# Where the places and the channels lie: the state of a long convolution, stored by channel pairs or by places

## The chip, the cores and the metric

The kernel runs on one core of a Trainium2 chip. The metric is the device time of one execution in microseconds: the median of three runs. A separate execution was recorded by the hardware profiler, and all views of the profile below come from that one.

## The reference

Two blocks stand one behind the other. The first is a long convolution over the sequence, computed through Fourier transforms for 4 batches of 12,480 places and 128 channels; the second is a feed-forward block with the gate `h * cos(h)` for the 49,920 rows that come out of it. Everything is float32.

```python
def _attn_ref(x, v, pos_emb, w1, w2):
    B, S, D = x.shape                       # 4, 12480, 128
    h_mlp = np.maximum(pos_emb @ w1, 0.0) @ w2
    window = np.exp(-0.01 * np.arange(S, dtype=np.float32))[:, None]
    h_filt = h_mlp * window
    u = x * v
    L = 2 * S
    Uf = np.fft.rfft(u, n=L, axis=1)
    Hf = np.fft.rfft(h_filt, n=L, axis=0)
    y = np.fft.irfft(Uf * Hf[None, :, :], n=L, axis=1)[:, :S, :]
    return (x * y).astype(np.float32)

def _moe_ref(x, w_in, w_out):               # 49920 x 128, d_ff 2048
    h = x @ w_in
    g = h * np.cos(h)
    return (g @ w_out).astype(np.float32)
```

## The kernel before

**The convolution** is a transform in two steps, with tables of sines and cosines as matrices (N1 = 96, N2 = 120). The state of one batch is one tile in SBUF, `slots`: partitions, 64 pairs of channels (`b`, CB = 64), 240 places (`j`), and the two channels of a pair (`i`). Its partition axis is the axis that the next step contracts, and each step overwrites it:

- *u*: `u_units` multiplies x and v (L437) and writes sums and differences of them into `slots` (`u_sums`, L447). On the way out of memory nothing is rearranged.
- *f1*: `f1_mm` (L455) takes, for one channel, 64 or 60 places of `slots` as the stationary operand and the table `c1` as the moving one, 192 columns. `f1_evict` copies the result of a channel pair back to 192 places of that pair (L467, mostly on ACT). For the filter `f1_evict_filter` writes to a tile of its own, `ftile` (L474), and to `above`, the upper places of `slots` (L476).
- *f2*: `f2_mm` takes a table `w` as the stationary operand and, for one place, all 128 channels of two complex parts as the moving one, 256 columns. `f2_product` multiplies with the filter's transform `h` and writes back to the place (L504 or L508, L510, L511). In the first batch the filter's f2 (L488, L491) runs beside it, and its result goes to memory as `hd` and is loaded for the later batches.
- *i1*: `i1_mm` takes for one channel 96 places (97 in the long stage) as the stationary operand and the table `cs` as the moving one, 120 columns. `i1_evict` writes 240 places of a channel pair (L531, L533; in the first batch for some pairs L524 and L527).
- *i2*: `i2_mm` takes a table `t` (in the trace `tm`) as the stationary operand and all 128 channels of a place as the moving one. `i2_out` multiplies by x (L555) and stores rows to `zd`.

**The feed-forward block** reads blocks of 128 rows by 4 places from `zd`, turns them (`moe_turn`), multiplies by `w_in` in 16 pieces of 512 columns (`moe_up`, ph), makes the gate on ACT and DVE (L810, L811, L816, L817) and multiplies by `w_out` with seven products in place of eight (`moe_sums` on POOL, `moe_down` at L842, acca and accb).

**Order.** The whole order is written out by hand. The first batch's filter, f1, f2 and i1 run alone (to about 303 us); after that the flag `tiled[0]` is set and the loop over (block, piece) asks a generator for one small step of the convolution behind every piece of the feed-forward block. So from then on i2 of a batch, u, f1, f2 and i1 of the next are spread between the matmuls of the feed-forward block. With the flag set `mm` (L136) splits the stationary operand of a matmul into columns 0 to 64 and the rest, and issues two matmuls to the two halves of the array:

```python
def mm(dst, left, right, start=True, stop=True):
    n = dst.shape[0]
    for lo, hi in ((0, CB), (CB, n)) if tiled[0] else ((0, n),):
        nc.tensor.matmul(dst[lo:hi], left[:, lo:hi], right, start=start, stop=stop)
```

f1 is always issued in two such halves (64 and 60 places). Each float32 matmul of the code appears in the profile as two MATMUL records, each with a LDWEIGHTS record of its own; the counts below are those of the records. In the profile's names `cv` is a PSUM bank of the convolution in the long stage, `ps` one in the first stage, `even` the tile that then holds `cs`, and `c` the tile `c1`.

`Between` hands out unused places of `slots` as work tiles before the first f1. `aT`, the hidden layer of the filter, lies in the upper places as well.

Of the kernel before, what the change touches and what calls it, by code (L numbers as in the profile page):

```python
# [10 lines left out]
F32 = mybir.dt.float32  # L11
# [7 lines left out]
P = 128  # L19
BANK = 512  # L20
# [14 lines left out]
def kernel(  # L35
# [46 lines left out]
    nc = tc.nc  # L82
# [4 lines left out]
    N1, N2 = 96, 120  # L87
# [5 lines left out]
    KE = ODD + H  # L93
# [3 lines left out]
    FR = 2 * (2 * N2 - 2 * N1)  # L97
    KF = N1 - 2 * (N2 - N1)
    CB = D // 2
# [13 lines left out]
    WCOL = 256  # L113

    dram = ctx.enter_context(tc.tile_pool(name="dram", bufs=1, space=DRAM))
    hd = dram.tile([N1 // 2, N2, 2, CB, 4], F32, name="hd")
    zd = dram.tile([NROWS, G, D], F32, name="zd")
    wd = dram.tile([N1 // 2, KE, 2, N2], F32, name="wd")
    td = dram.tile([N2 // G, N1, G, 2, R], F32, name="td")
# [13 lines left out]
# [4 lines that stand above are left out]
# [66 lines left out]
    class Tables:  # L203
        def __init__(self, pool, engine):
            self.pool, self.engine, self.waiting = pool, engine, []
            self.prod, self.moved = (
                pool.tile([P, P], F32, name=name) for name in ("prod", "moved"))
# [88 lines left out]
    class Between:  # L296


        def __init__(self, slots, first, last):
            self.places, self.used = slots[:, :, first:last, :], 0  # L300

        def tile(self, shape, dtype, name=None, bufs=1):
            n = 1 if len(shape) == 2 else shape[1]
            rows = self.places[0:shape[0], self.used:self.used + n].rearrange(
                "p b j i -> p b (j i)")[:, :, 0:shape[-1]]
            self.used += n
            return rows if len(shape) == 3 else rows[:, 0]

# [2 lines left out]
    def last_tables(pool):  # L311
        rows = pool.tile([N1, 4, R], F32, name="rows")

        tw_t = pool.tile([N1, 2, N2], F32, name="tw_t")
        return rows, tw_t
# [18 lines left out]
    def make_w(w, k1, **how):  # L334


        turn(w, even[:, 0, :], even[:, 1, :], tw_w[:, 0, k1:k1 + 1], tw_w[:, 1, k1:k1 + 1],
             **how)
# [52 lines left out]
    def filter_out(bank, aT, slots, j, w2_sb):  # L391

        ps = bank()
        for i, (jj, step) in enumerate(((H - 1 - j, 2), (j, 1))):
            nc.tensor.matmul(ps[0:FR, i * 2 * D:(i + 1) * 2 * D], aT[:, jj, 0:FR],
                             w2_sb[:, 0:step + 1:step, :], start=True, stop=True)
        pj = ps[0:FR, :].rearrange("p (n s b i) -> p s b n i", n=2, s=2, i=2)
        a = H - 2 - 2 * j
        for i in range(2):
            place = i * ODD + a  # L400
            nc.scalar.copy(out=slots[0:FR, :, place:place + 2, :], in_=pj[:, i])

    def n2s(g):

# [17 lines left out]
    def clear_gap(u):  # L422

        nc.gpsimd.memset(u[:, :, H:ODD, :], 0.0)
# [54 lines left out]
    def f2_mm(ps, w, k1, i, filt=False):  # L479


        k = k1 + i
        pi = ps[0:N2, :].rearrange("p (r b g i) -> p g r b i", r=2, g=2, i=2)[:, i]
        if not filt:
            mm(pi, w[:, i, :], parts[0:KE, :, k])
        elif k < KF:
            both = ftile[0:KE, :, k:k + N1 + 1:N1, :].rearrange("p b r i -> p r b i")
            nc.tensor.matmul(pi, w[:, i, :], both, start=True, stop=True)  # L488
        else:
            for r, src in enumerate((ftile[0:KE, :, k, :], above[0:KE, :, k - KF, :])):  # L490
                nc.tensor.matmul(pi[:, r], w[:, i, :], src, start=True, stop=True)  # L491

    def f2_product(pool, ps, h, k1, whole, engine=nc.gpsimd):


        y = parts[0:N2, :, k1:k1 + 2, :, :].rearrange("p r k b i -> p r b (k i)")
        t = pool.tile([N2, 2, CB, 4], F32, name="t", bufs=2)
        uu = ps[0:N2, :].rearrange("p (r b j) -> p r b j", r=2, j=4)
        if whole:
            for r, (dst, hh) in enumerate(((y, h[:, :, :, :]), (t[:, :, :, :], h[:, ::-1, :, :]))):  # L500
                u = uu[:, r]
                twice = bass.AP(tensor=u.tensor, offset=u.offset,
                                ap=[u.ap[0], [0, 2], *u.ap[1:]])
                nc.vector.tensor_tensor(dst, twice, hh, op=ALU.mult)  # L504
                yield
        for r, op in ((0, ALU.subtract), (1, ALU.add)):
            if not whole:
                nc.vector.tensor_tensor(y[:, r], uu[:, 0], h[:, r], op=ALU.mult)  # L508
                yield
                nc.vector.tensor_tensor(t[:, r], uu[:, 1], h[:, 1 - r], op=ALU.mult)  # L510
            (engine if r else nc.gpsimd).tensor_tensor(y[:, r], y[:, r], t[:, r], op=op)  # L511
            yield
# [127 lines left out]
    def f2_units(bank):  # L640
        with tc.tile_pool(name="there", bufs=3) as pool:
            ws, hs = {}, {}

            def before(j):
                ws[j] = pool.tile([KE, 2, N2], F32, name="w")
                nc.sync.dma_start(ws[j][:, :, :], wd[j, :, :, :])
                hs[j] = pool.tile([N2, 2, CB, 4], F32, name="h")
                nc.sync.dma_start(hs[j][:, :, :, :], hd[j, :, :, :, :])

            def mm(j, ps, i):  # L650
                if i == 0:
                    ps = bank()
                f2_mm(ps, ws[j], 2 * j, i)
                return ps

            yield from units(N1 // 2, F2_STEPS, before, mm,
                             lambda j, ps: f2_product(pool, ps, hs.pop(j), 2 * j, False), 4)

    def f2_both_units(bank):

        with tc.tile_pool(name="both", bufs=2) as pool:
            ws = {}

            def before(j):
                ws[j] = pool.tile([KE, 2, N2], F32, name="w")
                for i in range(2):
                    make_w(ws[j][:, i, :], 2 * j + i, half=bank)
                nc.sync.dma_start(wd[j, :, :, :], ws[j][:, :, :])
                if j == N1 // 2 - 1:
                    nc.sync.dma_start(cs[:, :, :], csd[:, :, :])  # L670

            def mm(j, ps, i):
                if i == 0:
                    ps = bank(), bank()
                for k in range(2):
                    f2_mm(ps[1 - i], ws[j], 2 * j, k, filt=i == 0)
                return ps

            def after(j, ps):
                h = pool.tile([N2, 2, CB, 4], F32, name="h", bufs=3)  # L680
                nc.scalar.activation(h[:, :, :, :].rearrange("p r b j -> p (r b j)"),
                                     ps[1][0:N2, :], AF.Copy, scale=1.0 / M)
                nc.sync.dma_start(hd[j, :, :, :, :], h[:, :, :, :])
                last = j == N1 // 2 - 1
                yield from f2_product(pool, ps[0], h, 2 * j, not last,
                                      nc.vector if last else nc.gpsimd)

            yield from units(N1 // 2, F2_STEPS, before, mm, after, 4, ahead=1)
# [201 lines left out]
    with tc.manual_schedule():  # L890
        with tc.tile_pool(name="psum", bufs=8, space=PSUM) as psum, \
                ExitStack() as first:
            def bank():
                return psum.tile([P, BANK], F32, name="ps")

            spool = ctx.enter_context(tc.tile_pool(name="slots", bufs=1))
            slots = spool.tile([P, CB, 2 * N2, 2], F32, name="slots")
            parts = slots[:, :, 0:2 * N1, :].rearrange("p b (r k) i -> p r k b i", r=2)
            above = slots[:, :, 2 * N1:2 * N2, :]
            aT = above.rearrange("p b j i -> p b (j i)")  # L900


            keep = tc.tile_pool(name="keep", bufs=1)
# [1 line left out]
            with tc.tile_pool(name="layers", bufs=1, side="right") as pool:  # L905
# [6 lines left out]
                for i in range(1, NCH):  # L912
                    pes[i] = filter_load(pool, i)
                    if i == 3:
                        for m in range(2):
                            for n in range(2):
                                nc.sync.dma_start(
                                    w2_sb[m * FO:(m + 1) * FO, (m + 1) * n, :], w2[:, :])
                between = Between(slots, KE, 2 * N1)
                vs = [between.tile([R, 2 * UA, D], F32).rearrange("p (h n) d -> p h n d", h=2)  # L920
                      for _ in range(5)]
                xpool = tc.tile_pool(name="x", bufs=5)
# [37 lines left out]
                nc.scalar.activation(c1[:, 2, :], c1[:, 0, :], AF.Copy, scale=-1.0)  # L960

            fpool = first.enter_context(tc.tile_pool(name="ftile", bufs=1, side="right"))
            ftile = fpool.tile([P, CB, N1 + KF, 2], F32, name="ftile")
            clear_gap(ftile[0:FR, :, :, :])
            for j in range(H // 2):
                filter_out(bank, aT, ftile, j, w2_sb)
# [36 lines left out]
            rows, tw_t = last_tables(wpool)  # L1003
# [64 lines left out]
        for i in range(len(steps) + LAG):  # L1068
# [5 lines left out]
            if i < len(steps):  # L1074
                n, c = steps[i]
# [52 lines left out]
```

## Time and profile before

| | |
|---|---|
| median of 3 runs | 3674.26 us (3673.73 to 3675.14) |
| the profiled execution's own time | 3673.78 us |
| its span, first to last instruction | 3671.2 us |
| mean granted clock of TensorE | 0.998 |
| busy DVE, POOL, ACT | 2811.3, 2757.7, 2229.7 us |
| MATMUL and LDWEIGHTS records | 40,810 each |
| DMA | 281.78 MB, mean 77 GB/s |

The profile is one execution. Engines: PE is TensorE's matmul, PEld its weight load, DVE is VectorE, ACT is ScalarE, POOL is GpSimd, SP issues the DMAs. A row of a group gives the source line, the engine and operation, out<-in by the program's names, the shapes, the count, then the busy time in us, the mean of one in ns, and the idle time before them with what ended it. For PE a shape such as 120*64 120x120 says: 120 partitions contracted, 64 columns of weights, 120 columns streamed. A row of the timeline gives the start in us, the time from the first start to the last end of the merged instructions, and their count. Matmuls are pipelined, so the length of one record is more than the pace at which they follow each other; the pace is the distance between starts.

In time, the parts of the profiled execution are: the filter and the f1 steps to about 145 us, both f2 of the first batch to about 245 us, i1 of the first batch from 245.6 to about 303 us, and then the long stage. In it, f1, f2, i1 and i2 of the later batches take turns.

### The profile page before, as it was taken

The numbers are of one execution on the slowest core, as the hardware profiler recorded it, in microseconds if no ns is written. First come the engines' busy times: TensorE is split into PE (matmuls) and PEld (weight loads), VectorE is DVE, ScalarE is ACT, GpSimd is POOL, SyncE is SP. The second block draws the span as 40 slices with busy tenths as digits, with TensorE's granted clock in tenths as the row PEclk, the third lists the DMA queues.
The fourth block names the chain that finished last, engine by engine and source line by source line (L and its number), as shares of the span: only waits on it lengthen the run. The fifth ranks groups of instructions, "written<-read, shape, count | busy, mean of one in ns | idle before, by whom it ended". The sixth has DMA issues, their size and how long they took to land.

```text
span 3671.2 us, 101732 instructions
## 1 busy us (share of the span) xinstructions
PE 3605.1 (98%) x40810; PEld 2553.1 (70%) x40810; DVE 2811.3 (77%) x5289; ACT 2229.7 (61%) x4482; POOL 2757.7 (75%) x3237
## 2 busy tenths in 40 slices
PE   8999999999999999999999999999999999999999
PEld 6777776666678776666677776766667786666666
DVE  7777885688887776688887776578887667777777
ACT  6657666656554556655655556665555446666666
POOL 7667996688864886688874887578884448878877
PEclk9999999999999999999999999999999999999999
DMA  7454540022213551022211562012220350000000
GB/s 193 123 159 134 161 136 26 23 70 72 73 42 102 163 148 29 22 71 71 71 37 47 162 172 69 13 53 74 68 72 16 91 166 22 19 24 19 19 25 14
DMA packets 219583, 281.78 MB, mean 77 GB/s; under 512 B 18778, under 2 KB 156514, under 8 KB 218986
## 3 DMA queue, kind: packets, MB, share of 16 engines
q1 hardware_dynamic: 219114, 275.29, 26.3%
q8 instruction: 324, 5.31, 0.6%
q14 instruction: 145, 1.19, 0.1%
HBM read 194.75 MB, written 80.46 MB: 75 GB/s over the span
## 4 chain that ended last, share of the span: by engine, by line
PE 85%; DVE 4%; ACT 1%; POOL 1%; issue 1%; DMA 0%; ACTq 0%; DVEq 0%; POOLq 0%; SPq 0%
PE ph L136 30%; PE cv L136 18%; PE accb L842 17%; PE acca L842 13%; PE cv L455 3%; PE cv L140 1%; DVE gt L817 1%; DVE gt L811 1%; PE ph L140 1%; ACT gt L810 1%; POOL ts L825 0%; DVE t L510 0%; ACT tile L873 0%; DVE slots L508 0%; POOL ts L828 0%
## 5 line engine op out<-in xcount | busy, mean ns | idle before, releaser
L810 ACT ACTIVATE gt<-ph 128x512 int32<-128x512 f32 (+1 forms) x1380 | 823.1, 596 | 1143.4 <-PE ph L136 1087.6
L811 DVE SCALAR_TENSOR_TENSOR gt<-ph,gt 128x512 f32<-128x512 f32 (+1 forms) x1380 | 948.2, 687 | 716.0 <-ACT gt L810 712.9
L825 POOL TENSOR_TENSOR ts<-gt 128x512 f32<-128x512 f32 (+2 forms) x784 | 1006.2, 1283 | 581.8 <-PE accb L842 566.1
L136 PE MATMUL ph<-at,w_in_sb 128*64 128x512 f32 (+1 forms) x5520 | 1426.4, 592 | 13.3 <-ACT tile L873 6.8
L816 ACT ACTIVATE gt<-gt 128x512 f32<-128x512 f32 (+1 forms) x1568 | 972.0, 620 | 3.5 <-DVE gt L811 2.8
L817 DVE TENSOR_TENSOR gt<-ph,gt 128x512 f32<-128x512 f32 (+1 forms) x1380 | 934.7, 677 | 0.0
L842 PE MATMUL accb<-ts,w_out_sb 128*64 128x128 f32 (+2 forms) x9408 | 649.8, 272 | 0.0
L829 POOL TENSOR_TENSOR ts<-gt,ts 128x256 f32<-128x256 f32 (+2 forms) x784 | 574.4, 733 | 61.5
L828 POOL TENSOR_TENSOR ts<-ts,gt 128x256 f32<-128x256 f32 (+2 forms) x784 | 574.3, 732 | 61.5
L842 PEld LDWEIGHTS acca<-gt,w_out_sb 128*64 128x64 f32 x6272 | 398.9, 137 | 267.4 <-issue 231.3
L842 PEld LDWEIGHTS accb<-ts,w_out_sb 128*64 128x64 f32 x9408 | 543.5, 137 | 0.0
L842 PE MATMUL acca<-gt,w_out_sb 128*64 128x128 f32 (+2 forms) x6272 | 479.3, 272 | 0.0
L842 PEld LDWEIGHTS accb<-gt,w_out_sb 128*64 128x64 f32 x3136 | 225.5, 137 | 253.9 <-issue 198.8
L136 PEld LDWEIGHTS ph<-at,w_in_sb 128*64 128x64 f32 x5520 | 353.6, 137 | 32.8 <-ACT tile L873 15.0
L511 POOL TENSOR_TENSOR slots<-slots,t 120x256 f32<-120x256 f32 x383 | 280.7, 739 | 122.8 <-DVE t L510 70.2
L136 PEld LDWEIGHTS cv<-slots,tm 96*64 96x64 f32 (+1 forms) x3840 | 243.6, 127 | 119.6 <-issue 114.3
L842 PE MATMUL accb<-gt,w_out_sb 128*64 128x128 f32 (+1 forms) x3136 | 311.2, 273 | 4.2 <-DVE ot L863 2.8
L842 PE MATMUL acca<-ts,w_out_sb 128*64 128x128 f32 (+1 forms) x3136 | 308.7, 272 | 1.4 <-POOL ts L828 1.2
L136 PE MATMUL cv<-slots,tm 96*64 96x128 f32 (+1 forms) x3840 | 274.7, 285 | 3.9 <-DVE slots L533 3.4
L136 PEld LDWEIGHTS cv<-even,slots 120*64 120x64 f32 (+1 forms) x3072 | 168.4, 125 | 60.8 <-issue 58.8
L842 PEld LDWEIGHTS acca<-ts,w_out_sb 128*64 128x64 f32 x3136 | 201.6, 137 | 2.4 <-POOL ts L828 2.1
L136 PE MATMUL cv<-slots,w 124*64 124x256 f32 (+1 forms) x1152 | 191.1, 406 | 1.9 <-ACT at L799 1.9
(136 smaller groups left out, 3741.0 us busy)
## 6 DMA issues: line engine op xcount, KB each, us to landing
h<-hd SPq DMA_DIRECT2D x144, 240.0 KB
tm<-td SPq DMA_DIRECT2D x96, 312.0 KB
xt<-in_x_dram SPq DMA_DIRECT2D x120, 208.0 KB
xs<-in_x_dram SPq DMA_DIRECT2D x120, 208.0 KB
zd<-xs SPq DMA_DIRECT2D x119, 208.0 KB
tile<-zd SPq DMA_DIRECT2D x96, 256.0 KB
vt<-in_v_dram SPq DMA_DIRECT2D x90, 208.0 KB
w<-wd SPq DMA_DIRECT2D x144, 116.2 KB
```

The source lines that it names most:

```text
L136: nc.tensor.matmul(dst[lo:hi], left[:, lo:hi], right, start=start, stop=stop)
L140: nc.tensor.transpose(dst, src, ident[0:n, 0:n])
L455: nc.tensor.matmul(dst[lo:hi], u[:, b, lo:hi, i], c1[0:u.shape[0], r:r + 2, :].rearrange("p r k -> p (r k)"), start=True, stop=True)
L511: (engine if r else nc.gpsimd).tensor_tensor(y[:, r], y[:, r], t[:, r], op=op)
L810: nc.scalar.activation(turns, ph[:, 0:m], AF.Identity, bias=phase)
L811: nc.vector.scalar_tensor_tensor(out=part, in0=ph[:, 0:m], scalar=phase, in1=turns, op0=ALU.add, op1=ALU.subtract)
L816: nc.scalar.activation(part, part, AF.Sin, scale=scale)
L817: nc.vector.tensor_tensor(part, ph, part, op=ALU.mult)
L825: nc.gpsimd.tensor_tensor(ts[:, 0:2, 0:half], gt[:, :, half:2 * half], gt[:, 0, 0:2 * half].rearrange("p (h n) -> p h n", h=2), op=ALU.sub ...
L828: nc.gpsimd.tensor_tensor(t[2], t[1], b11, op=ALU.add)
L829: nc.gpsimd.tensor_tensor(t[3], b21, t[2], op=ALU.subtract)
L842: nc.tensor.matmul(acc[h * CB:(h + 1) * CB, place, 0:r], w_out_sb[:, pair, weight, :], right[:, h * r:(h + 1) * r], start=(pair == 0 and i ...
```

## The change

The state becomes one tile of partitions, 240 places, 64 pairs, 2 channels: the 128 channels of a place stand side by side (512 bytes), and the places of a channel are 512 bytes apart. Before, the places of a pair were side by side (8 bytes from one to the next), and a place's pairs 1920 bytes apart. `ftile` is turned in the same way. `slots`, `parts` and `above` become views of the new tile with the old order of axes, so that most of the code that uses them stays as it is. The output of f2 in PSUM is written with the pairs of a place side by side, and `t`, `h` and `hd` follow that order. `aT` and the tiles of `Between` become plain contiguous rows. No instruction is added or taken away.

```diff
-    hd = dram.tile([N1 // 2, N2, 2, CB, 4], F32, name="hd")
+    hd = dram.tile([N1 // 2, N2, 2, BANK // 2], F32, name="hd")
...
-            self.places, self.used = slots[:, :, first:last, :], 0
+            self.places, self.used = slots[:, first:last, :, :].rearrange(
+                "p j b i -> p (j b i)").rearrange("p (a n) -> p a n", a=CB), 0
...
-            rows = self.places[0:shape[0], self.used:self.used + n].rearrange(
-                "p b j i -> p b (j i)")[:, :, 0:shape[-1]]
+            rows = self.places[0:shape[0], self.used:self.used + n, 0:shape[-1]]
...
-        pj = ps[0:FR, :].rearrange("p (n s b i) -> p s b n i", n=2, s=2, i=2)
+        pj = ps[0:FR, :].rearrange("p (n s b i) -> p s n b i", n=2, s=2, i=2)
...
-            nc.scalar.copy(out=slots[0:FR, :, place:place + 2, :], in_=pj[:, i])
+            nc.scalar.copy(out=slots[0:FR, :, place:place + 2, :].transpose([0, 2, 1, 3]),
+                           in_=pj[:, i])
...
-        pi = ps[0:N2, :].rearrange("p (r b g i) -> p g r b i", r=2, g=2, i=2)[:, i]
+        pi = ps[0:N2, :].rearrange("p (r g b i) -> p g r b i", r=2, g=2, i=2)[:, i]
...
-        y = parts[0:N2, :, k1:k1 + 2, :, :].rearrange("p r k b i -> p r b (k i)")
-        t = pool.tile([N2, 2, CB, 4], F32, name="t", bufs=2)
-        uu = ps[0:N2, :].rearrange("p (r b j) -> p r b j", r=2, j=4)
+        y = parts[0:N2, :, k1:k1 + 2, :, :].rearrange("p r k b i -> p r (k b i)")
+        t = pool.tile([N2, 2, BANK // 2], F32, name="t", bufs=2)
+        uu = ps[0:N2, :].rearrange("p (r n) -> p r n", r=2)
...
-            slots = spool.tile([P, CB, 2 * N2, 2], F32, name="slots")
-            parts = slots[:, :, 0:2 * N1, :].rearrange("p b (r k) i -> p r k b i", r=2)
+            state = spool.tile([P, 2 * N2, CB, 2], F32, name="slots")
+            slots = state[:, :, :, :].rearrange("p j b i -> p b j i")
+            parts = state[:, 0:2 * N1, :, :].rearrange("p (r k) b i -> p r k b i", r=2)
             above = slots[:, :, 2 * N1:2 * N2, :]
-            aT = above.rearrange("p b j i -> p b (j i)")
+            aT = state[:, 2 * N1:2 * N2, :, :].rearrange("p j b i -> p (j b i)").rearrange(
+                "p (a n) -> p a n", a=CB)
...
-                between = Between(slots, KE, 2 * N1)
+                between = Between(state, KE, 2 * N1)
...
-            ftile = fpool.tile([P, CB, N1 + KF, 2], F32, name="ftile")
+            ftile = fpool.tile([P, N1 + KF, CB, 2], F32, name="ftile")
+            ftile = ftile[:, :, :, :].rearrange("p j b i -> p b j i")
```

More of the change, by code (lines that the diff above doesn't have):

```diff
@@ L493, in f2_product @@
     def f2_product(pool, ps, h, k1, whole, engine=nc.gpsimd):
-        y = parts[0:N2, :, k1:k1 + 2, :, :].rearrange("p r k b i -> p r b (k i)")
-        t = pool.tile([N2, 2, CB, 4], F32, name="t", bufs=2)
-        uu = ps[0:N2, :].rearrange("p (r b j) -> p r b j", r=2, j=4)
+        y = parts[0:N2, :, k1:k1 + 2, :, :].rearrange("p r k b i -> p r (k b i)")
+        t = pool.tile([N2, 2, BANK // 2], F32, name="t", bufs=2)
+        uu = ps[0:N2, :].rearrange("p (r n) -> p r n", r=2)
         if whole:
-            for r, (dst, hh) in enumerate(((y, h[:, :, :, :]), (t[:, :, :, :], h[:, ::-1, :, :]))):
+            for r, (dst, hh) in enumerate(((y, h[:, :, :]), (t[:, :, :], h[:, ::-1, :]))):
                 u = uu[:, r]
@@ L646, in before @@
                 nc.sync.dma_start(ws[j][:, :, :], wd[j, :, :, :])
-                hs[j] = pool.tile([N2, 2, CB, 4], F32, name="h")
-                nc.sync.dma_start(hs[j][:, :, :, :], hd[j, :, :, :, :])
+                hs[j] = pool.tile([N2, 2, BANK // 2], F32, name="h")
+                nc.sync.dma_start(hs[j][:, :, :], hd[j, :, :, :])
             def mm(j, ps, i):
@@ L679, in after @@
             def after(j, ps):
-                h = pool.tile([N2, 2, CB, 4], F32, name="h", bufs=3)
-                nc.scalar.activation(h[:, :, :, :].rearrange("p r b j -> p (r b j)"),
+                h = pool.tile([N2, 2, BANK // 2], F32, name="h", bufs=3)
+                nc.scalar.activation(h[:, :, :].rearrange("p r n -> p (r n)"),
                                      ps[1][0:N2, :], AF.Copy, scale=1.0 / M)
-                nc.sync.dma_start(hd[j, :, :, :, :], h[:, :, :, :])
+                nc.sync.dma_start(hd[j, :, :, :], h[:, :, :])
                 last = j == N1 // 2 - 1
```

## The prediction

> **What bounds the kernel now.** I read the page first: parts 1 and 4, then the groups kept apart by shape, and last the timeline of TensorE inside the long stage.
>
> ```profile
> PE 3605.1 (98%) x40810; PEld 2553.1 (70%) x40810; DVE 2811.3 (77%) x5289; ACT 2229.7 (61%) x4482; POOL 2757.7 (75%) x3237
> PE 85%; DVE 4%; ACT 1%; POOL 1%; issue 1%; DMA 0%; ACTq 0%; DVEq 0%; POOLq 0%; SPq 0%
> ```
>
> TensorE is busy 98% of the span and carries 85% of the chain that ended last; no other engine is over 77%. So only what changes the pace of TensorE counts at once. That pace stands in the timeline, in the distance from the start of one row to the start of the next, divided by the count (rows of three stretches, about 750, 1055 and 1230 us, and one of 600 us):
>
> ```profile
> 600.24 0.82 PE L455 MATMUL cv<-c,slots 104*64 104x192 f32 x8
> 600.89 0.61 PE L842 MATMUL acca<-gt,w_out_sb 128*64 128x128 f32 x8
> ...
> 749.60 0.68 PE L136 MATMUL cv<-slots,w 124*56 124x256 f32 x4
> 750.10 0.40 PE L842 MATMUL accb<-gt,w_out_sb 128*64 128x128 f32 x4
> ...
> 1054.55 1.03 PE L136 MATMUL ph<-at,w_in_sb 128*64 128x512 f32 x4
> 1055.41 1.40 PE L136 MATMUL cv<-even,slots 120*64 120x120 f32 x24
> 1056.64 0.61 PE L842 MATMUL acca<-gt,w_out_sb 128*64 128x128 f32 x8
> ...
> 1230.64 1.17 PE L136 MATMUL cv<-slots,tm 96*40 96x128 f32 x16
> 1231.63 0.40 PE L842 MATMUL accb<-gt,w_out_sb 128*64 128x128 f32 x4
> 1231.85 0.83 PE L842 MATMUL accb<-ts,w_out_sb 128*64 128x128 f32 x12
> 1232.51 1.03 PE L136 MATMUL ph<-at,w_in_sb 128*64 128x512 f32 x4
> ```
>
> The two column halves that `mm` issues start 5 to 7 ns apart in the trace and run side by side, so a matmul costs half a pass here. From the starts in these rows: ph 0.86/4 = 215 ns, acc 0.66/12 = 55, i1 (cv<-even,slots) 1.23/24 = 51, f1 (cv<-c,slots) 0.65/8 = 81, f2 (cv<-slots,w) 0.50/4 = 125, i2 (cv<-slots,tm) 0.99/16 = 62. Over all their runs in the trace the medians are 214.5, 54.6, 51.4, 81.5, 120.8 and 61.3 ns. In columns per ns that is ph 2.39, acc 2.34, i1 2.33, f1 2.36, but f2 2.12 and i2 2.09. Only these two are slow, and only these two stream `slots` as the moving operand: 64 pieces of 8 bytes, 1920 bytes apart. In the first batch, where f2 runs as one tile of 120 columns, its pass takes 218 ns for the same 256 columns: 1.17 per ns, half of 2.35, so the pieces cost nothing there. They cost when two tiles stream at once.
>
> The weight loads are the other half of the reading:
>
> ```profile
> L136 PEld LDWEIGHTS ph<-at,w_in_sb 128*64 128x64 f32 x5520 | 353.6, 137 | 32.8 <-ACT tile L873 15.0 <-issue 7.0 <-PE ph L140 3.0
> L136 PEld LDWEIGHTS cv<-even,slots 120*64 120x64 f32 x1536 | 165.1, 138 | 22.9 <-issue 21.0 <-ACT ot L856 1.8
> L136 PEld LDWEIGHTS cv<-even,slots 120*33 120x33 f32 x1536 | 157.7, 111 | 37.9 <-issue 37.9
> L455 PEld LDWEIGHTS cv<-c,slots 104*64 104x64 f32 x768 | 105.9, 139 | 105.9 <-issue 66.9 <-ACT slots L467 13.9 <-ACT gt L816 13.3
> L136 PEld LDWEIGHTS ps<-even,slots 120*96 120x96 f32 x512 | 55.5, 174 | 3.4 <-POOL slots L511 3.4
> ```
>
> 64 weight columns take 137 ns side by side (ph) and 138 at 8 bytes' step (i1), so that step is free. From 33 to 64 columns is 27 ns more: 0.87 a column; the warm 96-column loads (167 ns in the trace; the row's 174 holds the cold ones) give 0.9. So a load is about 84 ns fixed and 0.83 to 0.87 ns a column, and a load starts 2 ns after the matmul before it. What must fit into a pass is the column time: 53 of 162 ns in f1, 53 of 102.5 in tiled i1, 80 of 102.5 in the first, untiled i1.
>
> **The change, part by part.** Instructions, their order, their waits and their counts stay as they are on every engine, SP and its queues included; `hd` keeps its bytes. Only steps in memory change, so no wait is added and nothing is queued anew.
>
> *f2 and i2 stream contiguous places.* Both should go to the pace of acc and ph. i2: 3840 x (61.3 - 54.6) = 25.7 us. For f2's 256 columns, between acc and ph on a line: 107.9 ns; 1152 x (120.8 - 107.9) = 14.9 us. Sum 40.6 us. The i2 of the first batch (a quarter, 6.4 us) runs in slices where TensorE is not quite full (18.3 to 20.0 of every 20 us between 320 and 540 us), so I let 38 us reach the end. If the pace has another cause than the 1920-byte pieces, it is 0. Untiled f2 gains nothing: 218 ns is the pace of its columns.
>
> *f1 and i1 load weights from places 512 bytes apart instead of 8.* No row has such a load. From below: no cost, 0.83 ns a column. A gain is excluded, since 8 bytes' step is as fast as none. From above, by the pieces: untiled f2 fetches one piece per 2 columns, 1.67 ns, free; two tiles in i2 take 122.6 ns for 64 pieces, 1.91 ns. If every weight column now costs such a fetch, it is 1.67 ns alone and 1.91 with a second tile. I take that, because separate pieces are the nearest thing to separate columns, and no row shows pieces coming faster; the range keeps 0.83.
> - First i1, 512 passes of 96 columns: 96 x 1.67 = 160 ns against 102.5. 481 of them run at that pace; the other 30 at 200 ns (the granted clock is 0.50 there) and hide it. 481 x 57.5 = 27.7 us. It lies on the path: PE is busy 55.7 of the 57 us there, DVE 38.7.
> - Tiled i1, 1536 passes of 64 and 33 columns: 33 at 1.91 while both load, 31 at 1.67 alone, 115 ns against 102.5. The first pass of each of 115 runs loads behind ph, so 1421 x 12.5 = 17.8 us (bounds 7 at 1.67 throughout, 28 at 1.91).
> - f1: 60 x 1.91 + 4 x 1.67 = 121 ns, under 162: nothing, in the stage and at the start alike. The cover is the pass of 192 columns; it is gone from 2.5 ns a column.
>
> On this the Trainium skill has a rule that speaks against the change ("SBUF — State Buffer", Door 1: The DMA port swizzle): full rate needs two hits on each 16-byte line, and every access that goes to a new line pays. Weights at 8 bytes have two hits on a line, at 512 one; the pairs of f2 and i2 have two and should be free, which untiled f2 bears out and the two tiles do not. It gives no size, so the sum above stands on rows.
>
> *Evictions of f1 and i1 now write pairs 512 bytes apart.* DVE wrote pairs 1920 bytes apart in L447: 411 ns at the least for 256 elements, and 408 at the least for the contiguous L510. POOL L447 has 749 against 735 contiguous. ACT wrote runs of four in L401, 369 ns for 256 elements, as L856 (263 for 128) would extrapolate. So nothing; at the 13% of the tiled streams it would be 60 ns on each of 256 ACT copies, 5 us of it open in the first f1, where ACT's 645 ns a unit stand beside PE's 650. Kept as a bound.
>
> *f2's products, the sums of u, the memory of hidden layers:* L504 is 682 beside 679 for its contiguous twin, L508 412 beside 413, POOL L511 739 beside 735. Nothing.
>
> Sum against the profiled execution (span 3671.2, its own time 3673.78, the median 3674.26): -38 + 27.7 + 17.8 = +7.5. Moved by the 0.5 between the two: 3682.
>
> **The rivals.** *The weights are nearly free.* If the limit is what two tiles fetch together, 2 pieces per 1.91 ns, a column costs 0.96: 96 columns 92 ns, tiled 93 ns, both under the 100 of the stream. Then -38 to -41: 3633 to 3636. The cost begins at 1.04 ns a column untiled and 1.56 tiled; up to 1.4 it is at most 481 x 32 = 15 us, so the kernel is still 23 us faster, 3652. For it: the loads at half clock (283 ns from the group's mean, against 167) show that the array and not memory sets 0.83. Against it: no row with pieces of 4 bytes. Chance 0.34, faster.
>
> One page prices such hops on another engine ("Vector Engine (DVE) Microarchitecture Reference", Measured stream behaviour on trn2): 1.73 ns instead of 1.05 for one element a hop. As an estimate from it, 1.73 ns per weight column would make first i1 31 us longer; by its ratio, 1.4 ns, it is the upper end of this rival. No row here shows it.
>
> *The two tiles' loads share one fetch* (slower). If the loads of both tiles come one after the other at 1.67, tiled i1 has 97 columns, 162 ns: 1421 x 59.5 = 85 us; f1 has 124, 207 ns against 162: 45 x 568 passes not behind ph = 26 us, and some 10 in the first f1s. With 27.7 and -38: +110, 3785. It decides from 1.03 ns a column in i1. For it: two streams hinder each other in f2 and i2. Against it: that hindrance is 13%, not 100%; and 64 and 60 columns load side by side in 139 and 135 ns. Chance 0.13.
>
> *The moving side gains nothing* because its pace has another cause (the partitions, 96 and 124, say; but f1 with 104 and i1 with 120 are at full pace): 3674 if the weights are free, 3720 if they cost what I take. Chance 0.09 (0.03 no change, 0.06 slower).
>
> **How the numbers follow.** The forecast, weights at one piece per column, has 0.44. Its bounds (tiled i1 at 7 or 28, the moving gain 36 to 41, ACT 0 to 5) give 3668 to 3699, on both sides of no change; about 0.2% (7 us) is what a measurement can tell. I split it 0.04 faster, 0.13 same, 0.27 slower. With the rivals: faster 0.04 + 0.34 = 0.38; same 0.13 + 0.03 = 0.16; slower 0.27 + 0.13 + 0.06 = 0.46. The range must reach from the free weights, 3632, through the forecast and the lost gain to 3740; above that lies most of the shared fetch, the rest that is left out.
>
> **What would show it.** Starts of cv<-slots,tm at 54.6 ns and cv<-slots,w at 108 would show the gain; unchanged, the third rival. Weight loads of cv<-even,slots 64 columns at 190 to 200 ns (now 138), of ps<-even,slots at about 247, and the first i1 at 85 us instead of 57 would show the cost; loads at 140 to 150 the first rival. cv<-c,slots must stay at 81.5 ns; at 100 or more the two tiles share a fetch. L533 at 395 and L467 at 473 must not move. I am wrong at the root if the new time sits in DVE, ACT or DMA.

## The result, and the profile after

The changed kernel takes 3712.43 us (median of 4 runs, 3710.54 to 3713.00) beside 3674.70 for the kernel before: a ratio of 1.0102, with a 95% interval of 1.0084 to 1.0119. It is slower by 38 us. The profiled execution has a span of 3709.0 us, 37.8 more than before, at the same mean granted clock of 0.998.

The page, parts 1 and 4, shows that the kind of bound has not changed:

```profile
PE 3639.4 (98%) x40810; PEld 2663.2 (72%) x40810; DVE 2845.7 (77%) x5289; ACT 2245.8 (61%) x4482; POOL 2756.1 (74%) x3237
PE 87%; DVE 6%; DMA 2%; POOL 2%; issue 2%; ACT 2%; DVEq 0%; SPq 0%; ACTq 0%; POOLq 0%
```

TensorE still fills 98%, and the weight loads (PEld) hold 110 us more than before, with the same count. The timeline of TensorE in the long stage, again read from start to start, shows where this went (line numbers in these rows are the old ones or one higher):

```profile
781.17 0.60 PE L136 MATMUL cv<-slots,w 124*64 124x256 f32 x4
781.61 0.39 PE L843 MATMUL accb<-gt,w_out_sb 128*64 128x128 f32 x4
...
1089.99 1.73 PE L136 MATMUL cv<-even,slots 120*33 120x120 f32 x23
1091.45 0.31 PE L843 MATMUL acca<-gt,w_out_sb 128*64 128x128 f32 x1
1091.55 0.28 PE L136 MATMUL cv<-even,slots 120*64 120x120 f32 x1
1091.60 0.56 PE L843 MATMUL acca<-gt,w_out_sb 128*64 128x128 f32 x6
...
1250.35 1.07 PE L136 MATMUL cv<-slots,tm 96*64 96x128 f32 x16
1251.22 0.64 PE L843 MATMUL acca<-gt,w_out_sb 128*64 128x128 f32 x8
```

f2 now needs 0.44/4 = 110 ns a matmul and i2 0.87/16 = 54: both are at the pace of the contiguous operands. i1 needs (1091.60 - 1089.99)/24 = 67 ns where it needed 51; over all its matmuls the mean is 64.2, and was 52.7. Its rows also show something that i1 had nowhere before: a matmul of acca starts, at 1091.45, before the last one of i1, at 1091.55. Before, the tiled i1 stood in 115 unbroken runs; now such matmuls break it into 229 pieces. The last to start is one of the half with 64 columns, so the half with 33 is ahead of it. The groups of the loads, kept apart by shape, show those weights:

```profile
L136 PEld LDWEIGHTS cv<-even,slots 120*64 120x64 f32 x1536 | 212.9, 222 | 11.3 <-issue 6.1 <-ACT ot L857 0.3
L136 PEld LDWEIGHTS cv<-even,slots 120*33 120x33 f32 x1536 | 178.2, 161 | 19.8 <-issue 0.4
L456 PEld LDWEIGHTS cv<-c,slots 104*64 104x64 f32 x768 | 146.9, 221 | 69.4 <-issue 41.7 <-ACT gt L817 12.1 <-ACT slots L468 11.9
L136 PEld LDWEIGHTS ps<-even,slots 120*96 120x96 f32 x512 | 85.6, 260 | 3.4 <-POOL slots L512 3.4
```

138 ns have become 222, 111 have become 161, 139 have become 221, and the 96-column load of the first batch is at 260. In f1 the longer load costs almost no time: its matmuls have a median of 81.6 ns (81.5 before), since a pass there lasts 162 ns.

The time between the first matmul of one stage and the first of the next, from the starts in both traces, gives the whole account:

| stage | before | after | difference |
|---|---|---|---|
| to the first f1, and both f1 of the start | | | +2.3 |
| first f2 | 100.3 | 100.5 | +0.2 |
| first i1 | 57.2 | 87.1 | +29.9 |
| i2 (four times) | 1536.8 | 1516.1 | -20.7 |
| f1 (three times) | 466.9 | 470.0 | +3.1 |
| f2 (three times) | 1003.3 | 991.9 | -11.4 |
| tiled i1 (three times) | 361.6 | 396.2 | +34.6 |

The last i2 row runs on to the end of the span. The sum is +38.0, against 37.8 between the spans.

DVE is busy 34 us longer, which the prediction named as a sign against it. 30 of them sit in the multiplication of x and v (before L437, now L438), 1013 ns a piece instead of 674, whose operands the change leaves as they were. The kernel "the moving side alone" below has the old layout and 1009 ns there, and is the faster one; so this is neither the layout nor the lost time.

### The profile page after: what moved, and what is told of

Read it like the earlier page. It is cut to its first block, busy times and chain, and to the rows that moved or that the text cites. A ratio compares the mean times of both kernels' runs of the same rounds, so it can differ in the third digit from the quotient of the medians.

```text
span 3709.0 us, 101730 instructions
## 1 busy us (share of the span) xinstructions
PE 3639.4 (98%) x40810; PEld 2663.2 (72%) x40810; DVE 2845.7 (77%) x5289; ACT 2245.8 (61%) x4482; POOL 2756.1 (74%) x3237
## 4 chain that ended last, share of the span: by engine, by line
PE 87%; DVE 6%; DMA 2%; POOL 2%; issue 2%; ACT 2%; DVEq 0%; SPq 0%; ACTq 0%; POOLq 0%
PE ph L136 30%; PE cv L136 17%; PE accb L843 17%; PE acca L843 13%; PE cv L456 3%; PE ps L136 2%; DMA wd<-w 2%; PE cv L140 1%; DVE gt L818 1%; DVE gt L812 1%; PE ps L456 1%; PE ph L140 1%; PE ps L395 1%; ACT gt L811 1%; POOL power L155 0%
## 5 line engine op out<-in xcount | busy, mean ns | idle before, releaser
L136 PE MATMUL ph<-at,w_in_sb 128*64 128x512 f32 (+1 forms) x5520 | 1444.0, 592 | 14.9 <-ACT tile L874 7.5
L843 PE MATMUL accb<-ts,w_out_sb 128*64 128x128 f32 (+2 forms) x9408 | 659.8, 272 | 0.0
L843 PE MATMUL acca<-gt,w_out_sb 128*64 128x128 f32 (+2 forms) x6272 | 489.6, 272 | 0.0
L136 PEld LDWEIGHTS ph<-at,w_in_sb 128*64 128x64 f32 x5520 | 363.1, 137 | 34.4 <-ACT tile L874 15.0
L843 PE MATMUL accb<-gt,w_out_sb 128*64 128x128 f32 (+1 forms) x3136 | 322.7, 274 | 4.5 <-DVE ot L864 3.2
L136 PEld LDWEIGHTS cv<-slots,tm 96*40 96x40 f32 (+1 forms) x3840 | 227.5, 127 | 117.9 <-issue 112.2
L136 PEld LDWEIGHTS cv<-even,slots 120*33 120x33 f32 (+1 forms) x3072 | 239.0, 192 | 31.2 <-issue 6.5
L136 PE MATMUL cv<-slots,tm 96*40 96x128 f32 (+1 forms) x3840 | 252.1, 274 | 3.7 <-DVE slots L534 3.2
L136 PE MATMUL cv<-even,slots 120*64 120x120 f32 (+1 forms) x3072 | 230.8, 288 | 0.0
L456 PEld LDWEIGHTS cv<-c,slots 104*64 104x64 f32 (+1 forms) x1536 | 150.2, 218 | 93.6 <-issue 65.5
```

What stands on the lines that cost most here:

```text
L456: nc.tensor.matmul(dst[lo:hi], u[:, b, lo:hi, i], c1[0:u.shape[0], r:r + 2, :].rearrange("p r k -> p (r k)"), start=True, stop=True)
L843: nc.tensor.matmul(acc[h * CB:(h + 1) * CB, place, 0:r], w_out_sb[:, pair, weight, :], right[:, h * r:(h + 1) * r], start=(pair == 0 and i ...
```

## The experiments

**Steps on constant tiles.** One kernel does none of the work. It issues runs of 12 matmuls of one kind, 24 passes, on constant tiles: first with weights at growing steps (one tile of 96 columns; two of 64 and 33; two of 64 and 60 under 192 streamed columns), then with contiguous weights and moving operands in pieces.

```diff
+    def weights(k, first, n, form):             # n columns, `form` words apart
+        a = big[0:k, :]
+        return bass.AP(tensor=a.tensor, offset=a.offset + first * form, ap=[a.ap[0], [form, n]])
...
+    for s in words:
+        go(f"one{4 * s}B", 120, (96,), s, 120, row)
+    for s in words:
+        go(f"two{4 * s}B", 120, (64, 33), s, 120, row)
...
+    for name, dims in forms:                    # [[h, 64], [1, 2]]: 64 pieces of 8 bytes, hop h words
+        go(f"mt_{name}_", 96, (64, 40), 1, 128, view(96, dims))
```

> This kernel does none of the reference's work: it only runs matmuls on constant tiles, 12 of each kind one behind the other, to measure the pace at which TensorE takes weights and moving operands at different steps in memory. Theory of the 16-byte line: a weight load costs about 0.83 ns a column while two columns share a line (steps of 4, 8 bytes) and 1.7 to 2.2 ns from 16 bytes on, the same for every larger step; 96 columns at 512 bytes then pace at about 170 ns (as the first i1 after the change), 64 and 33 side by side at about 120 to 130 ns a pass; 64 and 60 columns under 192 moving columns stay at 162 ns. Moving pieces of 8 bytes cost 12 to 14 ns a pass of 128 columns with two tiles and nothing with one, whatever the hop; pieces of 16 bytes or more cost nothing; single elements cost about twice the time. Rival, banks: the cost of both depends on the hop, is worst at 512, 1024 or 1920 bytes, and falls at 520, 528 or 1936 bytes; then padding would be enough. Rival, the tiles share one fetch: 64 and 33 columns at 512 bytes pace like 97 columns in one load, 170 ns or more.

The timeline of its TensorE, where the name before the arrow says the test (one = one tile, two = two tiles, then the step in bytes):

```profile
21.04 2.71 PE L42 MATMUL one8B<-plain,big 120*96 120x120 f32 x24
58.70 4.22 PE L42 MATMUL one512B<-plain,big 120*96 120x120 f32 x24
83.73 2.68 PE L42 MATMUL two8B<-plain,big 120*64 120x120 f32 x48
98.84 3.04 PE L42 MATMUL two64B<-plain,big 120*64 120x120 f32 x48
112.03 3.41 PE L42 MATMUL two512B<-plain,big 120*64 120x120 f32 x48
125.51 3.15 PE L42 MATMUL two1920B<-plain,big 120*64 120x120 f32 x48
128.73 4.12 PE L42 MATMUL fone8B<-plain,big 104*64 104x192 f32 x48
141.43 4.21 PE L42 MATMUL fone512B<-plain,big 104*64 104x192 f32 x48
```

24 passes of 120 streamed columns take 2.7 us at 8 bytes with one tile and with two, and 4.2 or 3.4 at 512; under 192 columns (fone) the step makes next to no difference, 162.5 ns a pass at 8 bytes and at 512. The moving operands have rows of their own: contiguous (mt_c), then pieces of 8 bytes at hops of 512, 1920, 1952 and 1984 bytes, two tiles each (the hop is not in the name; the rows follow the order of the code):

```profile
145.70 2.83 PE L42 MATMUL mt_c__950<-big 96*64 96x128 f32 x48
157.61 3.69 PE L42 MATMUL mt_r2h__1066<-big 96*64 96x128 f32 x48
165.12 3.18 PE L42 MATMUL mt_r2h__1124<-big 96*64 96x128 f32 x48
174.56 3.25 PE L42 MATMUL mt_r2h__1211<-big 96*64 96x128 f32 x48
177.88 2.86 PE L42 MATMUL mt_r2h__1240<-big 96*64 96x128 f32 x48
```

From the starts of the middle passes, in ns a pass:

| step of the weights, bytes | 4, 8 | 12 | 16 | 32 | 64 | 128 | 512, 1024 | 520 | 528 | 1920 |
|---|---|---|---|---|---|---|---|---|---|---|
| one tile, 96 columns | 102.5 | 131.1 | 176.7 | 180.0 | 165.0 | 166.7 | 166.7 | 186.7 | 176.7 | 166.7 |
| two tiles, 64 and 33 | 102.5 | 102.5 | 117.2 | 120.5 | 113.2 | 117.5 | 129.9 | 121.5 | 117.3 | 118.0 |

| moving pieces, 128 columns | contiguous | 16 bytes, five hops | 8 bytes, hop 16 | 64 | 512 | 1920 | 1936 | 1952 | 1984 | 2048 | 2304 |
|---|---|---|---|---|---|---|---|---|---|---|---|
| one tile | 109.2 | 109.2 | 115.6 | 109.3 | 110.0 | 111.7 | 113.3 | 126.7 | 110.0 | 110.0 | 110.0 |
| two tiles | 109.2 | 109.2 | 113.3 | 110.2 | 145.2 | 123.2 | 113.3 | 126.7 | 110.1 | 143.3 | 146.7 |

(1024 bytes reads 129.8 and 144.7 in the two-tile rows. With slow weights the two halves drift apart, so those two-tile values move by 1 to 3 ns with the passes that are taken. The later expectations use values up to 3 ns lower, from a reading that counted half a pass too many between the starts.) Three things follow. Up to 8 bytes a pass stays at the pace of its stream; from 16 bytes on a weight column costs about 1.7 to 2.0 ns with one tile (96 bytes, not in the table, is the dearest with 188.9 ns a pass); at 512 bytes it is 166.7/96 = 1.74. With two tiles the price depends on the step, and 512 bytes is among the dearest (256 and 1024 are equal to it). And 8-byte pieces of a moving operand are not dear as such: with two tiles they cost up to 37 ns at some hops and 1 ns at others. Single elements 16 or more bytes apart take 218 to 229 ns with one tile, about twice the contiguous pass as expected, and with two tiles up to 287, at 512 bytes. The theory of the line has the size right for the weights, and is wrong where it said "the same for every larger step" and "whatever the hop": there the rival that looks at the hop is nearer, but 1920 bytes is not among the worst. The tiles do not share one fetch: 97 columns would take as long as the 96 of one tile.

**The moving side alone.** The kernel before, with contiguous moving operands for f2 and i2 in the long stage.

```diff
-            mm(pi, w[:, i, :], parts[0:KE, :, k])
+            src = parts[0:KE, :, k]
+            if tiled[0] and k1:
+                src = w_in_sb[0:KE, 0:2 * D]
+            mm(pi, w[:, i, :], src)
...
-                mm(ps[0:R, i * D:(i + 1) * D], t[:, i, r, :], slots[0:N1, :, place, :],
+                src = slots[0:N1, :, place, :] if g == 0 else w_in_sb[0:N1, 0:D]
+                mm(ps[0:R, i * D:(i + 1) * D], t[:, i, r, :], src,
```

> The kernel before with one edit: in the long stage the moving operands of f2 and i2 (all but the first of each batch) are contiguous columns of w_in_sb instead of the places of slots; weights, evictions and the layout stay as before, so this part of the result is left out. Theory (TensorE reads 8-byte pieces slowly when two tiles stream): i2 goes from 61.3 to 54.6 ns and f2 from 120.8 to 108 ns a matmul, and the whole by what these stages gained after the change, about 21 + 11 us: 3643 us. Rival, the pairs that f2 writes to PSUM are what costs in f2: f2 stays at 120.8 and only i2's 21 us come, 3654. Rival, the pace has another cause (partitions, order): 3674.

It took 3642.80 us, a ratio of 0.9916 (0.9901 to 0.9930) to the kernel before, which took 3673.55 beside it: 31 us less, as expected. The ratios below are to the kernel before as well. In its trace f2 is at 108.8 ns in the median and i2 at 54.7, while f2 still writes its pairs to PSUM 16 bytes apart. So the reading was what cost, not the writing. The groups of the two (PE, by shape), first as they were before, then in this run:

```profile
L136 PE MATMUL cv<-slots,tm 96*64 96x128 f32 x1920 | 271.6, 285 | 3.9 <-DVE slots L533 3.4 <-ACT at L799 0.5
L136 PE MATMUL cv<-slots,w 124*64 124x256 f32 x576 | 187.1, 406 | 1.9 <-ACT at L799 1.9
...
L136 PE MATMUL cv<-w_in_sb,tm 96*64 96x128 f32 x1856 | 239.2, 273 | 0.8 <-ACT at L803 0.5 <-DMA tm<-td 0.3
L136 PE MATMUL cv<-w_in_sb,w 124*64 124x256 f32 x564 | 169.3, 381 | 1.9 <-ACT at L803 1.9
```

**The weights of i1 alone.** The kernel after, with i1's weights at a step of 8 bytes.

```diff
-               slots[0:N2, b, r * N1:r * N1 + n, i], cs[:, r, :])
+               slots[0:N2, b, r * N1:r * N1 + n, i] if b == 0 else
+               cs.rearrange("p r k -> p (r k)")[:, 0:2 * n:2], cs[:, r, :])
```

> The kernel after with one edit: i1 takes its weights (all channel pairs but the first) from the table cs at a step of 8 bytes instead of from the state at 512 bytes; evictions, i2, f1 and f2 stay as after, so this part of the result is left out. Theory (weight columns 512 bytes apart load slowly and i1 cannot cover it): first i1 goes back from 87 to 57 us, tiled i1 from 64 to 53 ns a matmul, 30 + 35 us in all: 3648 us, which is faster than before by the gain of f2 and i2. Rival, i1 is slower because its evictions write pairs 512 bytes apart (DVE and ACT hold it up): no change, 3712.

It took 3647.16 us, a ratio of 0.9929 (0.9912 to 0.9945), 65 us less than the kernel after. The loads, in the groups by shape, are where they were before the change:

```profile
L136 PEld LDWEIGHTS cv<-even 120*64 120x64 f32 x1512 | 162.3, 138 | 13.7 <-issue 11.4 <-ACT ot L858 1.8
L136 PEld LDWEIGHTS ps<-even 120*96 120x96 f32 x504 | 53.4, 171 | 0.0
```

The first i1 stage is back at 56.4 us (57.2 before), and the three tiled ones at 87.9, 125.8 and 148.3, within 0.2 of the kernel before. The evictions, which still write their pairs 512 bytes apart, therefore cost i1 nothing that shows.

**The weights of f1 alone.**

```diff
-            nc.tensor.matmul(dst[lo:hi], u[:, b, lo:hi, i],
+            left = u[:, b, lo:hi, i]
+            if b:
+                left = c1[0:u.shape[0]].rearrange("p r k -> p (r k)")[:, 0:2 * (hi - lo):2]
+            nc.tensor.matmul(dst[lo:hi], left,
```

> The kernel after with one edit: f1 takes its weights (all channel pairs but the first) from the table c1 at a step of 8 bytes instead of from the state at 512 bytes, so this part of the result is left out. Theory: f1's longer loads (221 ns after, 139 before) lie under passes of 162 ns; only 2 to 5 us come back, from the first pass of runs and the two f1 steps at the start: 3707 to 3711. Rival, f1's loads push the stages around them too: 3700 or less.

It took 3711.83 us, a ratio of 1.0103 (1.0088 to 1.0118), no different from the kernel after: the 2 to 5 us that were expected back did not come clear of the noise. The three long f1 stages went from 158.2, 156.0 and 155.8 us to 157.9, 155.6 and 155.3. At the start the two f1 take 92.8 us instead of 94.8, but the f2 behind them 1.8 us more. So the weights' part in the long f1 stages is about 1 us; the rest of the +3.1 in the table is not from its weights, for the kernel with the moving side alone, whose f1 is untouched, also has 157.5 in the first of them (before: 156.1).

**The same step at another price.** To see in the kernel itself that the step counts, and not only that there is one: i1's weights in the long stage at 64 bytes.

```diff
+               w_in_sb[0:N2, 0:16 * n:16] if b and tiled[0] else
                slots[0:N2, b, r * N1:r * N1 + n, i], cs[:, r, :])
```

> The kernel after with one edit: in the long stage i1 takes its weights (all channel pairs but the first) from w_in_sb at a step of 64 bytes instead of from the state at 512, so this part of the result is left out; the first i1 stays as after. Theory (the price of a weight column with two tiles hangs on the step: 112.9 ns a pass at 64 bytes on constant tiles, 129.6 at 512): tiled i1 falls from 64.2 to about 57 ns a matmul, 1421 passes x 16.7 ns = 24 us, 3688 us. Rival, every step of more than 8 bytes costs the same (one line per column): no change, 3712.

It took 3693.80 us, a ratio of 1.0052 (1.0035 to 1.0069): 18.6 us less than the kernel after, where 24 were expected. The load of 64 columns takes 203 ns instead of 222, and a matmul 58.7 ns in the mean (64.2 after, 57 expected):

```profile
L136 PEld LDWEIGHTS cv<-even,w_in_sb 120*64 120x64 f32 x1512 | 189.8, 203 | 11.3 <-issue 5.4 <-ACT ot L858 1.4
```

So the rival, one price for every step over 8 bytes, is out; the size on constant tiles was right to about three quarters.

**Another hop for the old layout.** If hops are dear or cheap by their length, the layout before needs only another hop. The pairs' stride was lengthened by more places; f1 and i1 keep their step of 8 bytes. In the versions with 4 and 8 places more, the room is made by putting as many of the filter's upper places into them.

```diff
-            slots = spool.tile([P, CB, 2 * N2, 2], F32, name="slots")
+            slots = spool.tile([P, CB, 2 * N2 + 8, 2], F32, name="slots")     # + 2, + 4, + 8
...
-    KF = N1 - 2 * (N2 - N1)
+    KF = N1 - 2 * (N2 - N1) - 8                                              # 4, 8 places alone
...
-            above = slots[:, :, 2 * N1:2 * N2, :]
+            above = slots[:, :, 2 * N1:2 * N2 + 8, :]                        # 4, 8 places alone
```

> The kernel before, whole, with 8 unused places behind the 240 of each pair: a place's pairs lie 1984 bytes apart instead of 1920, and the places stay 8 bytes apart. For the room, 8 of the filter's upper places move from ftile into the new ones, and tw_w is given back after f2. Theory (moving pieces clash by the hop, and 1984 is free, 107.8 ns a pass on constant tiles): i2 at 54 to 55 ns and f2 at 108 to 110 ns a matmul, weight loads of i1 and f1 at 138 ns as before, in all the 31 us of the moving side without the price of the weights: 3640 to 3645 us, the fastest version. Rival, pieces of 8 bytes cost with two tiles whatever the hop: 3674.

> The kernel before, whole, with 2 unused places per pair: the hop is 1936 bytes. Theory (111.2 ns a pass on constant tiles, against 121.6 at 1920 and 107.1 contiguous): i2 near 55.6 ns, f2 near 111, together 22 to 27 of the 31 us: 3647 to 3652. Rival, pieces cost whatever the hop: 3674.

> The kernel before, whole, with 4 unused places per pair, and 4 of the filter's upper places in them: the hop is 1952 bytes. It is the counter-proof: 124.2 ns a pass on constant tiles, no better than 1920's 121.6. Theory: i2 at 62 to 63 ns, f2 near 122, 3674 to 3681. Rival, any padding helps, or the room and order that it changes: 3650 or less.

| hop, bytes | time, us | ratio (95%) | i2, ns | f2, ns | first f2, us |
|---|---|---|---|---|---|
| 1920 (before) | 3674.78 | | 61.3 | 120.8 | 100.3 |
| 1936 | 3654.05 | 0.9943 (0.9929 to 0.9956) | 57.4 | 114.5 | 100.4 |
| 1952 | 3690.71 | 1.0043 (1.0029 to 1.0057) | 63.2 | 125.2 | 108.0 |
| 1984 | 3646.99 | 0.9924 (0.9911 to 0.9938) | 55.9 | 110.5 | 100.4 |

With 1984 bytes the whole kernel runs 28 us faster than before and 65 us faster than after: nearly all of the moving side's gain, without the price of the weights. It is 2 us over the upper end of what was expected, with i2 at 55.9 instead of 54 to 55. Its groups by shape show both sides at once, the moving operands at or near the means of the contiguous ones (273 beside 273, 387 beside 381) and the loads at the old 138:

```profile
L135 PE MATMUL cv<-slots,tm 96*64 96x128 f32 x1920 | 251.5, 273 | 3.9 <-DVE slots L532 3.4 <-ACT at L798 0.5
L135 PE MATMUL cv<-slots,w 124*64 124x256 f32 x576 | 176.6, 387 | 1.9 <-ACT at L798 1.9
L135 PEld LDWEIGHTS cv<-even,slots 120*64 120x64 f32 x1536 | 165.0, 138 | 22.9 <-issue 21.0 <-ACT ot L855 1.8
```

1936 came out 2 us over the upper end of its expectation too. 1952 is the counter-proof and went further than expected, 3691 instead of 3674 to 3681. The table of constant tiles had most of the reason: at 1952 even a single tile pays, 126.7 against 111.7 ns, which I had not put into the expectation. The first f2 runs as one tile and lost 7.7 us. Its group in the profile, before and in this run:

```profile
L136 PE MATMUL ps<-slots,w 124*120 124x256 f32 x192 | 49.4, 377 | 0.0
...
L136 PE MATMUL ps<-slots,w 124*120 124x256 f32 x192 | 56.1, 415 | 0.0
```

## Why the prediction was right, and where it was not

The forecast was slower by 7.5 us, at the bound of what can be told; measured is 38. The direction, the outer range of 3632 to 3740 and every mechanism of the sum held; one term had clearly the wrong size, so that 3712 lies 13 us beyond the 3668 to 3699 that the forecast gave its own mechanism. That the sign came out is in part luck: 7.5 is the small rest of a gain of 38 and a cost of 45.5, and an error as large as the one made, the other way, would have turned it.

- *f2 and i2 at the contiguous pace*: forecast 54.6 and 107.9 ns, measured 54.7 and 108.8. Of the 40.6 us I let 38 reach the end; the stages gained 32.1. The gain per matmul was right and the share that arrives too high. The three later i2 gained 6.1 to 6.3 us each, as forecast; the first gained 2.0 of its 6.4. TensorE is idle for 11.5 us there (about 2 in each of the next two), and for 12.9 after, which accounts for a part; the rest is open, like the 3.5 us that f2 gained less than its 14.9. Shown by the moving side alone, 31 us.
- *The first i1*: forecast 160 ns a pass and 27.7 us; constant tiles give 166.7, the stage lost 29.9. Right.
- *Tiled i1*: this is the term that was mis-sized. Forecast 17.8 us, with bounds 7 and 28 (its own price of 1.67 gives 6, not 7); measured 34.6, beyond the upper one. Its price came from the nearest row, pieces of a moving operand at 1920 bytes with two tiles, and gave 115 ns a pass. Weights at 1920 bytes do take 118 on constant tiles. At 512 bytes they take 129.9, and 1421 x 27.4 = 39 us is 4 over what came. In the kernel itself a step of 64 bytes instead of 512 gave back 18.6 us. What failed is the tacit step that a hop is a hop: the row's price was carried over to a hop of another length. Both bounds had been taken from that one hop.
- *f1*: forecast covered by the 162 ns of its pass, with the cover gone from 2.5 ns a column. A load of 64 columns went to 221 ns and the pass stayed; about 1 us is f1's. Right.
- *Evictions*: DVE L534 has 399 and 408 ns (395 and 398 before), ACT L468 494 and 507 (473 and 481): 1 to 3% on DVE and 4 to 5% on ACT, where I had put nothing, and 13% as a bound. It shows in no stage of the long part: with 8-byte weights i1 is back, and the second and third f1 are too. At the start the two f1 stages and what lies ahead of them are 2.3 us longer; that f1 stretch differs by 1.5 us between kernels that have the same code there (93.7 before, 92.2 with the moving side alone), so it stays open whether ACT had a part in it.

The rival with nearly free weights fell with the first row of loads. It leaned on the load following the array's clock, which can say who sets the pace at 8 bytes, but not who sets it at 512. The rival in which both tiles share a fetch forecast 162 ns in i1 and a longer f1; neither came: i1 has 2 x 64.2 = 128 ns. The rival without a moving gain fell with i2 at 54.7.

The rule of the Trainium skill that spoke against the change ("SBUF — State Buffer", Door 1: The DMA port swizzle: two hits on each 16-byte line, and a price for each new line) agrees with the weights: 102.5 ns at 4 and 8 bytes, 176.7 at 16. Read as two hits on a line, it would have every hop of the moving pairs free, as two words share a line. The runs differ: 110 ns at 1984 bytes, but 123 at 1920 and 145 at 512 with two tiles. The estimate from the Trainium skill's "Vector Engine (DVE) Microarchitecture Reference", Measured stream behaviour on trn2, 1.73 ns for each hopping element on another engine, comes very near the 1.74 ns per weight column with one tile.

## What to carry to other kernels

A layout has two readers on TensorE, the stream and the weight load, and each has a pass to hide in: price both, per stage, before turning a tile around. In these runs a weight load with a step of 16 bytes or more needed 1.7 ns a column or more, so it was free only where the streamed columns last longer (192 here, not 120). When a strided operand is slow, try another stride first: 64 more bytes per channel pair brought 28 of the 32 us that the turned layout gained in its streams, and no other stage became longer, while 32 bytes made it worse. And a price read from one stride holds for that stride.

## What the hardware showed that I had not expected

- With two tiles streaming, the cost of 8-byte pieces goes by the hop in a pattern: 143 to 147 ns a pass at 512, 1024, 2048 and 2304 bytes (all multiples of 256), 123 and 124 at 1920 and 2176 (odd multiples of 128), 110 at 64 and 1984 (odd multiples of 64), 113 at 16 and 1936; contiguous is 109.2. The divisor is not all of it: 32 and 1952 bytes, both odd multiples of 32, have 115 and 126.7. Pieces of 16 bytes cost nothing at any of the five hops tried. What lies behind the pattern stays open.
- With one tile the pattern is another: 110 ns at the multiples of 256, 115.6 at 16 and 126.7 at 1952.
- The two column halves of a pair of matmuls need not stay together. On constant tiles at 512 bytes the half with 33 columns has a median of 103 ns between its starts, the pace of the stream, while the half with 64 has 140. In the kernel one half goes on to the next product while the other is behind: the last i1 matmul shows up between rows of the next group (acca at 1091.45, i1 at 1091.55).
